# Three block products between the last layer norm's power and its use, and the third chunk's blocks fetched while the last chunk is normalised

## The chip, the cores and the metric

The kernel runs on one core of a Trainium2 chip. A core has five engines that each work through their own queue in order: TensorE (PE; its weight loads are shown as PEld), VectorE (DVE), ScalarE (ACT), GpSimd (POOL) and SyncE (SP), which issues the transfers. The metric is the device time in microseconds (us) of one execution; less is better. The kernel before took 570.78 us as the median of three runs (569.49 to 571.22).

## The reference

A transformer block on 2048 tokens of width 512, in float32: a modulated layer norm, linear attention with 32 heads, a residual, a second modulated layer norm, and a feed-forward part in which two projections to 1376 columns are multiplied and projected back.

```python
x = A_x
mod = (_silu(c) @ w_mod).reshape(c.shape[0], 6, 1, -1)
sa, ca, ga, sb, cb, gb = (mod[:, 0], mod[:, 1], mod[:, 2], mod[:, 3], mod[:, 4], mod[:, 5])
h = _layernorm(x, axis=-1) * (1 + ca) + sa
x = x + ga * _A_ref(h, A_wqkv, A_wo)
h = _layernorm(x, axis=-1) * (1 + cb) + sb
x = x + gb * _B_ref(h, B_w_gate, B_w_up, B_w_down)
...
def _B_ref(x, w_gate, w_up, w_down):
    g = jnp.einsum("bsd,df->bsf", x, w_gate)
    u = jnp.einsum("bsd,df->bsf", x, w_up)
    h = g * u
    return jnp.einsum("bsf,fd->bsd", h, w_down)
```

## The kernel before

The 2048 tokens are four chunks of 512, each of four tiles of 128 tokens. Every float32 matmul is done as three: each operand is split into a rounded high part and the low part that is left over, and the products high x high, high x low and low x high are added in PSUM. A split (L182 to L184) is a rounding copy on ScalarE and a subtraction on VectorE or GpSimd; it gives two tiles.

The attention runs first, chunk by chunk. Behind it stands the feed-forward part, in which the eleven column blocks f of 128 of the two projections are handled in two ways. The last three blocks (`lone`) are plain products for chunks 0 and 1. The first eight, and for chunks 2 and 3 all eleven, are done for two chunks at once by a scheme of Strassen's kind, in which seven products take the place of eight. `block` (L856 to L904) is one such block: it writes into four PSUM banks a, b, c, d and is a generator that stops after each product. The products stand in the order p1 (bank a), p5 (d), p6 (b), p2 (a), p7 (c), p3 (d), p4 (c); each is six matmuls of 128 x 512 at L838. Between them stand copies from bank to bank or to a tile on ScalarE (L843): a to b after p1, d to a tile after p5, b to c and b to a tile after p6; additions on VectorE: L893 after p7, L897 after p3; and two multiplications (L866), of bank a after p3 and of bank c after p4. The product of p1 of the next block goes into bank a again. The results of these multiplications are split in the next block after its p1 (`flush`), into tiles kh and kl.

The list `at` in `ffn` (L972 to L1013) hangs other work on the points: at p6 the scaling of the down weights (L985); at p7 the loads of the weights two blocks ahead, and the splits of the weights of the next block (`high` on ScalarE, L817 and L820, four operations; `lows` on GpSimd, L824, four operations); at p3 the split of the down weights; at p4 on GpSimd the sums of the weights two blocks ahead (L806, four operations). After some blocks a group of products with the down weights follows (L914 to L916), and VectorE adds its results to x (L678).

There are 19 such blocks, numbered from 0 in the order in which they run. Blocks 0 to 7 are for chunks 0 and 1, blocks 8 to 18 for chunks 2 and 3. The first two run mixed with the end of the attention and with the second layer norm of the last chunk: `fill(n)` advances the generator by n products, and the lines of the main program between the calls of `fill` set the order of everything else (L1142 to L1165). After that nothing is called by hand and the generator runs to its end (L1168 to L1170).

The layer norm of the last chunk, in its pieces: `y_b(15)` takes the last statistics; `rstd_of` adds epsilon on VectorE (L233) and raises to the power -1/2 on GpSimd (L234); `nmr_of` multiplies the mean by it on VectorE (L237); `xhat` normalises a tile on ScalarE (L243); `ln2_turn` transposes two columns of blocks on TensorE (L250), scales and shifts them on ScalarE (L262) and writes them to DRAM (`kept`, L264).

The left operands of blocks 8 to 18 come from chunks 2 and 3. `Left` (L743 to L779) loads four blocks of them from `kept` for each of two values of k: a11 and a12 of the third chunk, a21 and a22 of the fourth. `sum` makes s1 = a21 + a22, s3 = a11 - a21, s2 = s1 - a11 and s4 = a12 - s2 on VectorE (L756), `split` splits seven of them (ScalarE, then VectorE at L184), and `aside` writes both parts to DRAM (L772), from where `fetch` reads them shortly before block 8. These are 4 sums and 7 splits for each k, 22 steps in the list `trickle`; `some` takes one of them at each of the points p1, p5, p2, p3 and p4 of blocks 2 to 6, where block 2 begins with p2 (L992).

All buffers of a row of 128 x 512 come from one pool of 99, and transfers of one queue are issued by SP in order; a transfer whose buffer or source is not ready holds those behind it.

Of the kernel before, what the change touches and what calls it, by code (L numbers as in the profile page):

```python
# [22 lines left out]
def tile_adaln_block(  # L23
# [42 lines left out]
    def f32(ap):  # L66
        return ap.bitcast(F32)
# [7 lines left out]
    def B(tag, shape=(P, D), dt=F32):  # L75

        return T(tiles, tag, shape, dt)
# [30 lines left out]
    def load(src, tag):  # L108
        raw = B(tag, (P, *src.shape[1:]))[:src.shape[0]]
        nc.sync.dma_start(raw, src)  # L110
        return raw
# [70 lines left out]
    def split(src, h, l, low=None):  # L182
        nc.scalar.activation(h, src, AF.Copy)  # L183
        (low or nc.vector).tensor_tensor(l, src, f32(h), op=ALU.subtract)  # L184

    def split_raw(raw, shape=(P, D), low=None):
        h = B("w", shape, F32R)
        l = B("w", shape, F32R)
        split(raw, h[:raw.shape[0]], l[:raw.shape[0]], low)
        return h, l  # L190
# [23 lines left out]
    class Norm:  # L214
        def __init__(self, tiles):
            self.tiles = tiles
            self.mv = T(small, "mv", (P, NJ, 2))
            self.n = [None] * NJ
            self.ps = [None] * KD
            self.t = [None] * KD  # L220
# [312 lines left out]
    for k in range(KD):  # L533
        f = B("n")
# [81 lines left out]
    def y_b(i):  # L616
        ch, j = divmod(i, NJ)
        ps = yps.pop(i)
        nc.scalar.activation(xts[ch][j], ps, AF.Copy)
        norm2[ch].stats(j, of=ps)  # L620
# [106 lines left out]
    def ln2_turn(ch, *ks, cast=None):  # L727
        norm2[ch].transpose(*ks)
        norm2[ch].modulated(cb, sb, *ks, keep=kept[ch], cast=cast, parts=ch in PLAIN)
# [3 lines left out]
    kept = [[tc.dram_tile([P, D], F32, name=f"kept_{ch}_{k}") for k in range(KD)] for ch in range(NCH)]  # L733
# [6 lines left out]
    KH = KD // 2  # L740
    SIDE = ("a11", "s1", "s2", "a12", "s3", "a22", "s4")

    class Left:  # L743


        def __init__(self, cs, k):
            self.k = k
            self.f = {n: load(kept[c][kk], "f") for n, c, kk in (("a21", cs[1], k), ("a22", cs[1], KH + k),
                                                               ("a11", cs[0], k), ("a12", cs[0], KH + k))}

        def sum(self, *names):
            for n in names:
# [5 lines left out]
        def split(self, *names, low=None):  # L758
            for n in names:
                h, l = B("h", dt=F32R), B("h", dt=F32R)  # L760
                split(self.f.pop(n), h, l, low)
                self.done(n, h, l)

        def into(self, side):
# [10 lines left out]

        def steps(self):

            todo = [lambda n=n: self.sum(n) for n in ("s1", "s3", "s2", "s4")]
            return todo + [lambda n=n: self.split(n) for n in SIDE]  # L779

    def fetch(stash, side, *names):
        for n in names:
            side[n] = []
            for k in range(KH):
                side[n].append(tuple(B("h", dt=F32R) for _ in range(2)))
                for part, x in enumerate(side[n][k]):
                    nc.sync.dma_start(f32(x), stash[n, k, part])

    def plain_side(cs):
        t = [norm2[c].t for c in cs]  # L790
        return {"a11": t[0][:KH], "a12": t[0][KH:], "a22": t[1][KH:]}
# [58 lines left out]
    todo = []  # L850

    def flush():
        while todo:
            todo.pop(0)()

    def block(A, R, out, at):  # L856


        n, R = R.n, R.of
        a, b, c, d = (x[:n] for x in banks)  # L860

        def T2(tag):
            return B(tag)[:n]

        def mul(ps, x):
            nc.vector.tensor_tensor(x, ps, x, op=ALU.mult)  # L866
            todo.append(lambda: out.append(split_h(x, n)))

        def also(point):
            for do in at.get(point, ()):  # L870
                do()

        times(a, A["a11"], R["b11"], True)
        copy(b, a)
        flush()
        also("p1")
        yield
        times(d, A["s1"], R["t1"], True)
        p5 = T2("u")
        copy(p5, d)  # L880
        also("p5")
        yield
        times(b, A["s2"], R["t2"], False)
        copy(c, b)
        u2 = T2("u")
        copy(u2, b)
        also("p6")
        yield
        times(a, A["a12"], R["b21"], False)
        also("p2")  # L890
        yield
        times(c, A["s3"], R["t3"], False)
        nc.vector.tensor_tensor(p5, c, p5, op=ALU.add)  # L893
        also("p7")
        yield
        times(d, A["s4"], R["b22"], False)
        nc.vector.tensor_tensor(u2, d, u2, op=ALU.add)  # L897
        mul(a, u2)
        also("p3")
        yield  # L900
        times(c, A["a22"], R["t4"], False)
        mul(c, p5)
        also("p4")
        yield  # L904
# [36 lines left out]
    def right_load(n):  # L941
        if n < len(steps):
            rights[n] = Right(steps[n][1])

    def right_sums(n, on=None):
        if n < len(steps):
            rights[n].sums(on)

    def right_split(n, on=None):
        if n < len(steps):  # L950
            rights[n].high()
            rights[n].lows(on)
# [3 lines left out]
    def draw_load(n):  # L956
        if n < len(steps):
            f0, k = fts[steps[n][1]]
            draws[n] = load(w_down[f0:f0 + k, :], "raw")

    trickle = []

    def some(count):
        for _ in range(min(count, len(trickle))):
            trickle.pop(0)()
# [6 lines left out]
    def ffn():  # L972

        first_side, second_side = side, {}
        m = 0
        for g, (cs, fs) in enumerate(groups):
            last = g + 1 == len(groups) or groups[g + 1][0] != cs
            outs, ds = [], []
            A = first_side if cs == (0, 1) else second_side
            for f in fs:  # L980
                out = []
                draw = draws.pop(m)

                def scale(d=draw):
                    nc.vector.tensor_tensor(d, d, gb[:d.shape[0]], op=ALU.mult)  # L985

                at = {"p6": [scale],
                      "p7": [lambda: draw_load(m + 1), lambda: right_load(m + 2), lambda: right_split(m + 1)],
                      "p3": [lambda: ds.append(split_raw(draw, low=nc.gpsimd))],
                      "p4": [lambda: right_sums(m + 2)]}  # L990
                for point in ("p1", "p5", "p2", "p3", "p4")[2 if m == 2 else 0:]:
                    at.setdefault(point, []).append(lambda: some(some_at.get(m, 0)))  # L992
                if m + 1 < len(steps) and steps[m + 1][0] != cs:
                    at["p1"].append(lambda: fetch(stash, second_side, "a11", "s1"))
                    at["p7"].insert(0, lambda: fetch(stash, second_side, "s2", "a12", "s3"))
                elif m and steps[m - 1][0] != cs:
                    at["p1"].append(lambda: fetch(stash, second_side, "s4", "a22"))
                outs.append(out)
                yield from block(A, rights[m], out, at)
                m += 1  # L1000
                if free[0] and parts:
                    takes = [down_group(*p) for p in parts.pop(0)]
                    yield
                    for take in takes:
                        take()
            cut_at = {2: ([[0, 1, 2, 3], []], [[], [0, 1, 2, 3]]),
                      3: ([[0, 1, 2], []], [[3], [0, 1]], [[], [2, 3]])}[len((groups + groups[-1:])[g + 1][1])]
            parts.extend([(ch, i, js, outs, ds, last) for i, (ch, js) in enumerate(zip(cs, jss)) if js] for jss in cut_at)
        flush()
        while parts:  # L1010
            group = parts.pop(0)
            for p in group:
                down_group(*p, by_tile=not parts, end=not parts and p is group[-1])()  # L1013

    def fill(n):
        for _ in range(n):
            next(work, None)
# [70 lines left out]
    y_step(9)  # L1088
    side.update(plain_side((0, 1)))
    first = [Left((0, 1), k).into(side) for k in range(KH)]  # L1090
    right_load(0)
    right_load(1)
    g = gate_up(1, f0)
# [45 lines left out]
    draw_load(0)  # L1139
    stash, some_at = {}, {m: 1 for m in range(2, 7)}  # L1140
    work = ffn()
    y_step(14, seed=None)  # L1142
    fill(1)
# [8 lines left out]
    fill(2)  # L1152
    y_b(15)
    norm2[3].rstd_of()
    norm2[3].nmr_of()
    fill(2)
    norm2[3].xhat(0)
    fill(2)
    norm2[3].xhat(1)
    fill(1)  # L1160
# [2 lines left out]
    ln2_turn(3, 0, 1)  # L1163
    fill(1)
    ln2_turn(3, 2, 3)  # L1165
    for k in range(KH):
        trickle += Left((2, 3), k).aside(stash).steps()
    free[0] = True  # L1168
    for _ in work:
        pass  # L1170
# [27 lines left out]
```

## Time and profile before

| | |
|---|---|
| median of the runs | 570.78 us (569.49 to 571.22) |
| profiled execution | 570.02 us |
| its span, first to last instruction | 568.3 us |
| matmuls (PE) busy | 560.3 us, 99% |
| VectorE, ScalarE, GpSimd busy | 66%, 49%, 33% |
| transfers, mean | 104 GB/s |

The profile is one execution. In its timeline each row has the start and the length in us, the engine, the line of the program, the operation, output and inputs, the shapes and a count; in square brackets stands the idle time of the engine just before, with what ended it. In the chain of waits each row has start, length, engine, tile and line. SPq is SP's queue of transfers. Where a row counts several instructions, the length runs from the first start to the last end.

### The profile page before, as it was taken

The page shows a single profiled execution, that of the slowest core. Times are in us where ns is not written, and L with a number is a line of the kernel's source. Part 1 is how long each engine was busy: PE and PEld are TensorE (multiplying, and loading weights), DVE is VectorE, ACT ScalarE, POOL GpSimd, SP SyncE. Part 2 cuts the span into 40 slices and gives each one's busy share as a digit, 9 for nine tenths or more (in the row PEclk, how much of TensorE's full clock was granted, in tenths as well). Part 3 has the DMA queues.
Part 4 walks back from the last instruction along what each step waited for, and adds up shares of the span by engine and source line. Part 5 has one row for each costly group of instructions (what it writes and reads, how often), then busy time and mean ns, then how long its engine had stood idle before and what let it go on. Part 6 is the DMA issues. An engine that isn't in the chain of part 4 may idle for free.

```text
span 568.3 us, 7356 instructions
## 1 busy us (share of the span) xinstructions
PE 560.3 (99%) x2575; PEld 458.8 (81%) x2575; DVE 373.1 (66%) x614; ACT 279.8 (49%) x500; POOL 186.2 (33%) x191
## 2 busy tenths in 40 slices
PE   8999999999999999999989999999999999999997
PEld 6778888888888878878878888787888888888886
DVE  7876868868768876759767777745554434344445
ACT  3785857546456546445865545534333333334110
POOL 2000000000011300000579666665667446556200
PEclk9999999999999999999999999999999999999999
DMA  8900223302301000804208553599336012200004
GB/s 289 374 3 2 74 75 110 114 0 62 93 0 47 29 1 37 260 0 149 57 2 277 180 190 104 202 348 330 115 111 178 26 57 55 57 19 2 0 1 148
DMA packets 50309, 59.34 MB, mean 104 GB/s; under 512 B 6432, under 2 KB 27168, under 8 KB 50272
## 3 DMA queue, kind: packets, MB, share of 16 engines
q1 hardware_dynamic: 50272, 58.87, 32.1%
q8 instruction: 20, 0.33, 0.2%
q14 instruction: 17, 0.14, 0.1%
HBM read 43.12 MB, written 15.73 MB: 104 GB/s over the span
## 4 chain that ended last, share of the span: by engine, by line
PE 89%; DMA 3%; issue 2%; POOL 1%; DVE 1%; ACT 1%; SPq 1%; POOLq 0%; ACTq 0%
PE bank L838 28%; PE acc L914 6%; PE acc L915 6%; PE acc L916 6%; PE acc L614 6%; PE bank L198 5%; PE bank L196 5%; PE bank L197 5%; PE acc L329 3%; PE acc L327 3%; PE acc L328 3%; PE bank L693 2%; PE bank L691 2%; PE bank L692 2%; PE bank L250 2%
## 5 line engine op out<-in xcount | busy, mean ns | idle before, releaser
L838 PE MATMUL bank<-h,w 128*128 128x512 f32 (+1 forms) x798 | 185.5, 390 | 1.8 <-ACT bank L843 1.2
L838 PEld LDWEIGHTS bank<-h,w 128*128 128x128 f32 (+1 forms) x798 | 148.2, 186 | 35.3 <-ACT bank L843 1.7
L843 ACT ACTIVATE bank<-bank 128x512 f32<-128x512 f32 (+1 forms) x38 | 22.1, 583 | 144.8 <-PE bank L838 144.8
L678 DVE TENSOR_TENSOR x<-acc,x 128x512 f32<-128x512 f32 (+1 forms) x73 | 49.1, 684 | 49.0 <-PE acc L916 48.2
L824 POOL TENSOR_TENSOR w<-raw,w 128x256 fp32r<-128x256 f32 (+3 forms) x38 | 42.4, 1117 | 106.4 <-ACT w L817 86.4
L184 POOL TENSOR_TENSOR w<-raw,w 128x512 fp32r<-128x512 f32 (+1 forms) x25 | 34.9, 1399 | 116.0 <-DVE mv L226 87.6
L914 PE MATMUL acc<-w,kh 128*128 128x512 f32 (+2 forms) x154 | 59.6, 387 | 0.0
L915 PE MATMUL acc<-w,kh 128*128 128x512 f32 (+2 forms) x154 | 59.6, 387 | 0.0
L916 PE MATMUL acc<-w,kl 128*128 128x512 f32 (+2 forms) x154 | 59.5, 386 | 0.0
L234 POOL TENSOR_TENSOR rstd<-ve,half 128x4 f32<-128x4 f32 (+1 forms) x9 | 9.4, 1044 | 126.0 <-DVE ve L233 124.5
L184 DVE TENSOR_TENSOR kl<-u,kh 128x512 fp32r<-128x512 f32 (+1 forms) x38 | 26.8, 746 | 33.1 <-ACT kh L183 31.2
L824 POOL TENSOR_TENSOR w<-t,w 128x512 fp32r<-128x512 f32 (+1 forms) x38 | 48.4, 1293 | 0.0
L196 PE MATMUL bank<-w,h 128*128 128x512 f32 x112 | 45.0, 402 | 0.0
L198 PE MATMUL bank<-w,h 128*128 128x512 f32 x112 | 43.9, 392 | 0.0
L197 PE MATMUL bank<-w,h 128*128 128x512 f32 x112 | 43.6, 389 | 0.0
L614 PE MATMUL acc<-w,xh 128*128 128x512 f32 x120 | 38.1, 399 | 0.0
L914 PEld LDWEIGHTS acc<-w,kh 128*128 128x128 f32 (+1 forms) x154 | 28.9, 188 | 6.0
L916 PEld LDWEIGHTS acc<-w,kl 128*128 128x128 f32 (+1 forms) x154 | 28.9, 188 | 5.9
L915 PEld LDWEIGHTS acc<-w,kh 128*128 128x128 f32 (+1 forms) x154 | 28.9, 188 | 5.9
L893 DVE TENSOR_TENSOR u<-bank,u 128x512 f32<-128x512 f32 (+1 forms) x19 | 13.1, 690 | 30.0 <-PE bank L838 30.0
L243 ACT ACTIVATE n<-x,nmr,rstd 128x512 f32<-128x512 f32 x32 | 24.1, 804 | 17.2 <-DVE nmr L237 15.9
L262 ACT ACTIVATE f<-bank,col,col 128x512 f32<-128x512 f32 x28 | 20.7, 775 | 14.5 <-PE bank L250 12.4
(177 smaller groups left out, 1105.1 us busy)
## 6 DMA issues: line engine op xcount, KB each, us to landing
raw<-in_w_mod_dram SPq DMA_DIRECT2D x24, 256.0 KB, 3.7
raw<-in_B_w_down_dram SPq DMA_DIRECT2D x20, 256.0 KB, 2.9
raw<-in_B_w_gate_dram SPq DMA_DIRECT2D x36, 128.0 KB, 3.7
raw<-in_B_w_up_dram SPq DMA_DIRECT2D x36, 128.0 KB, 3.6
x<-in_A_x_dram SPq DMA_DIRECT2D x16, 256.0 KB, 5.4
kept<-f SPq DMA_DIRECT2D x16, 256.0 KB, 2.0
f<-kept SPq DMA_DIRECT2D x16, 256.0 KB, 4.8
side_s<-h SPq DMA_DIRECT2D x16, 256.0 KB, 2.6
```

Source lines behind the costliest of these rows:

```text
L184: (low or nc.vector).tensor_tensor(l, src, f32(h), op=ALU.subtract)
L196: nc.tensor.matmul(ps, ah, bh, start=i == 0, stop=False)
L197: nc.tensor.matmul(ps, ah, bl, start=False, stop=False)
L198: nc.tensor.matmul(ps, al, bh, start=False, stop=i == n - 1)
L243: nc.scalar.activation(self.n[j], self.tiles[j], AF.Identity, scale=self.rstd[:, j:j + 1], bias=self.nmr[:, j:j + 1])
L614: nc.tensor.matmul(yps[i], x, y, start=False, stop=k == KD - 1 and x is al, skip_group_check=True)
L678: nc.vector.tensor_tensor(xt[:, a:b], dn[j][:, a:b], xt[:, a:b], op=ALU.add)
L824: sub = lambda out, x, y: (on or nc.gpsimd).tensor_tensor(out, x, f32(y), op=ALU.subtract)
L838: mm = lambda x, y, **kw: nc.tensor.matmul(ps, x[:, k], y, skip_group_check=True, **kw)
L914: nc.tensor.matmul(ps, hh[:, a:b], dh[:n, c:d], start=i == 0, stop=False)
L915: nc.tensor.matmul(ps, hh[:, a:b], dl[:n, c:d], start=False, stop=False)
L916: nc.tensor.matmul(ps, hl[:, a:b], dh[:n, c:d], start=False, stop=i == len(hs) - 1)
```

## The change

Three edits. The main program calls `fill(3)` between `rstd_of` and `nmr_of` of the last norm and `fill(1)` behind `nmr_of`, where it called `fill(2)` once; so 16 products rather than 14 are called by hand before the 22 steps begin. `Left` no longer loads when it is made: `get` does, and for the third and fourth chunk a11 and a12 are fetched behind the first `xhat`, a21 and a22 at the place where all were fetched. The 22 steps are put in another order: first the four splits of a11 and a12, then for each k the sums and the other splits, and one of the five points moves from p2 to p6.

```diff
+            self.of = {"a21": (cs[1], k), "a22": (cs[1], KH + k), "a11": (cs[0], k), "a12": (cs[0], KH + k)}
+            self.f = {}
+
+        def get(self, *names):
+            for n in names:
+                c, k = self.of[n]
+                self.f[n] = load(kept[c][k], "f")
...
-                split(self.f.pop(n), h, l, low)
+                split(self.f[n], h, l, low)
...
-            todo = [lambda n=n: self.sum(n) for n in ("s1", "s3", "s2", "s4")]
-            return todo + [lambda n=n: self.split(n) for n in SIDE]
+            late = [lambda n=n: self.sum(n) for n in ("s1", "s3", "s2", "s4")]
+            late += [lambda n=n: self.split(n) for n in SIDE if n not in ("a11", "a12")]
+            return [lambda n=n: self.split(n) for n in ("a11", "a12")], late
...
-                for point in ("p1", "p5", "p2", "p3", "p4")[2 if m == 2 else 0:]:
+                for point in ("p1", "p5", "p6", "p3", "p4")[2 if m == 2 else 0:]:
...
     first = [Left((0, 1), k).into(side) for k in range(KH)]
+    for x in first:
+        x.get("a21", "a22", "a11", "a12")
...
     norm2[3].rstd_of()
+    fill(3)
     norm2[3].nmr_of()
-    fill(2)
+    fill(1)
     norm2[3].xhat(0)
+    second = [Left((2, 3), k).aside(stash) for k in range(KH)]
+    for x in second:
+        x.get("a11", "a12")
     fill(2)
     norm2[3].xhat(1)
...
     ln2_turn(3, 2, 3)
-    for k in range(KH):
-        trickle += Left((2, 3), k).aside(stash).steps()
+    for x in second:
+        x.get("a21", "a22")
+    for part in zip(*[x.steps() for x in second]):
+        for todo_k in part:
+            trickle += todo_k
     free[0] = True
```

More of the change, by code (lines that the diff above doesn't have):

```diff
@@ L747, in __init__ @@
             self.k = k
-            self.f = {n: load(kept[c][kk], "f") for n, c, kk in (("a21", cs[1], k), ("a22", cs[1], KH + k),
-                                                               ("a11", cs[0], k), ("a12", cs[0], KH + k))}
+            self.of = {"a21": (cs[1], k), "a22": (cs[1], KH + k), "a11": (cs[0], k), "a12": (cs[0], KH + k)}
[4 more added lines that the diff above has]
+                self.f[n] = load(kept[c][k], "f")
         def sum(self, *names):
```

## The prediction

> **What bounds the kernel now.** I read four views in this order: the page's busy shares, TensorE's own waits, the chain of work that ended last, and the timeline of each engine around the last layer norm.
>
> ```profile
> span 568.3 us, 7356 instructions
> ...
> PE 560.3 (99%) x2575; PEld 458.8 (81%) x2575; DVE 373.1 (66%) x614; ACT 279.8 (49%) x500; POOL 186.2 (33%) x191
> ...
> L838 PE MATMUL bank<-h,w 128*128 128x512 f32 (+1 forms) x798 | 185.5, 390 | 1.8 <-ACT bank L843 1.2 <-DVE u L866 0.3 <-DVE u L893 0.3
> ```
>
> TensorE is busy for 99% of the span, and the change leaves its 2575 matmuls as they are. A gain can only be idle time, and the third line shows that the block products (L838) idle at three places, 1.8 us in all. I look at these places next, since every edit lies there.
>
> ```profile
> 280.68 4.24 PE L838 MATMUL bank<-h,w 128*128 128x512 f32 x18
> ...
> 285.23 5.72 PE L838 MATMUL bank<-h,w 128*128 128x512 f32 x24 [0.31 <-DVE u L866]
> ...
> 292.19 3.02 PE L838 MATMUL bank<-h,w 128*128 128x512 f32 x12 [1.24 <-ACT bank L843]
> ...
> 298.09 9.83 PE L838 MATMUL bank<-h,w 128*128 128x512 f32 x42
> ...
> 313.20 9.68 PE L838 MATMUL bank<-h,w 128*128 128x512 f32 x42
> ```
>
> The last row is an undisturbed block: 42 matmuls whose last takes 0.39 us, so one starts every (9.68 - 0.39)/41 = 0.227 us. I count the loss from start to start, which also holds the slow first matmuls after a wait. After the 18 matmuls from 280.68 the next was due at 280.68 + 18 x 0.227 = 284.77 and came at 285.23: 0.46 us lost at the hand-over from block 0 to block 1. After the 24 from 285.23 it was due at 290.68 and came at 292.19: 1.51 us lost. The first edit touches this wait. The chain of waits tells where it comes from:
>
> ```profile
> 287.46 1.02 POOL rstd L234
> 288.50 0.69 DVE nmr L237
> 289.19 0.61 DVE u L866
> ...
> 290.37 0.80 ACT n L243
> 291.17 0.48 ACT u L843
> 291.64 0.50 ACT bank L843
> ...
> 292.19 3.02 PE bank L838 x12
> ```
>
> ```profile
> 283.67 0.69 DVE L897 TENSOR_TENSOR u<-bank,u 128x512 f32<-128x512 f32 x1 [0.74 <-PE bank L838]
> ...
> 284.39 0.69 DVE L866 TENSOR_TENSOR u<-bank,u 128x512 f32<-128x512 f32 x1
> ...
> 285.94 0.34 DVE L233 TENSOR_SCALAR ve<-mv 128x4 f32<-128x4 f32 x1
> ...
> 288.50 0.69 DVE L237 SCALAR_TENSOR_TENSOR nmr<-mv,rstd 128x4 f32<-128x4 f32 x1 [2.23 <-POOL rstd L234]
> ...
> 286.95 0.58 ACT L843 ACTIVATE bank<-bank 128x512 f32<-128x512 f32 x1 [3.43 <-PE bank L838]
> ...
> 289.83 0.63 ACT L183 ACTIVATE kh<-u 128x512 fp32r<-128x512 f32 x1 [1.76 <-DVE u L866]
> ...
> 291.10 1.17 POOL L806 TENSOR_TENSOR t<-raw,t 128x256 f32<-128x256 f32 x1
> ```
>
> VectorE reaches the tiny nmr operation with 2.23 us to wait, because GpSimd runs the power (L234) behind the low parts of a weight. Behind nmr stands block 0's second product on VectorE (L866), behind that the second kh on ScalarE, behind that the first normalised tile (L243) and two copies; the second copy fills the bank of block 1's p7.
>
> **The change, part by part.** *The power's three products* (p4 of block 0, p1 and p5 of block 1) now stand between L234 and nmr. On VectorE L866 follows L233 directly, at 286.3. The kh pair follows on ScalarE's 286.95 copy, at 287.4 and 288.0. The copy of p5's bank then starts at 288.5, and the copy for p7 needs only p6: its last matmul starts at 285.23 + 17 x 0.227 = 289.09, and by the 286.95 copy (p1's last matmul starts at 286.37) a copy starts 0.58 later: 289.67, done 290.25. TensorE wants it at 290.68, so the 1.51 us go, with 0.4 us to spare. nmr itself now runs behind the two kl subtractions. Even if these take the 1.97 us they take today it is issued near 290.3, and ScalarE's copies hold the first normalised tile until 290.7 anyway; so nmr costs nothing there.
>
> ```profile
> 289.72 1.97 DVE L184 TENSOR_TENSOR kl<-u,kh 128x512 fp32r<-128x512 f32 x2
> ...
> 292.54 2.21 ACT L243 ACTIVATE n<-x,nmr,rstd 128x512 f32<-128x512 f32 x3
> ...
> 294.66 0.41 ACT L817 ACTIVATE w<-raw 128x256 fp32r<-128x256 f32 x1
> ...
> 294.96 1.14 ACT L820 ACTIVATE w<-t 128x512 fp32r<-128x512 f32 x2
> ...
> 297.05 2.77 ACT L262 ACTIVATE f<-acc,col,col 128x512 f32<-128x512 f32 x4
> ```
>
> *What becomes late next: the hand-over from block 1 to block 2.* The calls that advance the products rise from 14 to 16, so p4 of block 1 and p1 of block 2 now follow each other with no transposes between, as at block 0 to 1 today. The bank of p1 is read by L866, which waits for L897, which waits for p3. Today: L897 starts 0.49 after p3's last matmul (280.68 + 11 x 0.227 = 283.18), L866 0.72 later, TensorE 0.84 after that. After the change p7 starts at 290.68, p3's last matmul at 290.68 + 11 x 0.227 = 293.18; that gives 293.67, 294.39 and 295.23, where p1 was due at 290.68 + 18 x 0.227 = 294.77. New loss: 0.46 us, and all of TensorE's queue stands behind it. Today's run from p7 to block 2 (292.19 to 298.09) held the same 18 matmuls and both groups of transposes: 5.90 - 18 x 0.227 = 1.81 us of transposes, which now come inside block 2.
>
> *ScalarE between p7 of block 1 and p7 of block 2* has the tightest cover. From 290.7 it runs one tile (0.70 each, from the 2.21 row), four high parts (0.30 from L817's start to L820's, then 3 x 0.52 from the 1.14 row, the third part not before GpSimd's L806 ends at 292.27), a tile, a weight's high part (0.52) and two tiles: done at 296.1, where the transposes start at 295.23 + 6 x 0.227 = 296.59. Then come a copy at 296.95 (0.49, from the starts in the chain), two kh (0.52 as the high parts), four L262 (0.67 each, from the 2.77 row) with a copy among them (0.49), and the copy that block 2's p7 needs: issued 301.65, done 302.23, wanted at 295.23 + 24 x 0.227 + 1.81 = 302.49. Cost 0, margin 0.26; one more ScalarE operation of 0.5 would cost 0.25.
>
> *The early fetch.* Four loads of 256 KB move ahead of block 1's weight loads on SP's queue, and four stay behind the writes of the last normalised blocks.
>
> ```profile
> 275.66 0.46 SPq L800 DMA_DIRECT2D raw<-in_B_w_up_dram  x1
> ...
> 300.26 4.20 SPq L110 DMA_DIRECT2D f<-kept  x8
> ...
> 304.80 0.77 DVE L756 TENSOR_TENSOR s<-f,f 128x512 f32<-128x512 f32 x1 [0.38 <-DMA f<-kept]
> ...
> 300.84 0.74 POOL L806 TENSOR_TENSOR t<-raw 128x256 f32<-128x256 f32 x1
> ...
> 304.56 0.38 SPq L110 DMA_DIRECT2D raw<-in_B_w_down_dram  x1
> ...
> 312.03 0.75 POOL L806 TENSOR_TENSOR t<-raw 128x256 f32<-128x256 f32 x1
> ```
>
> SP issued block 1's weights by 275.66 and GpSimd took them at 300.84; four more issues of about 0.5 us are hidden by 20 us. The 0.38 us wait of VectorE for the first sum goes, but TensorE did not wait for it: worth 0. The last L262 moves from 299.8 to 301.7, so the remaining loads end near 306 and block 2's weight loads follow them, 2 us later than 304.56. GpSimd took these at 312.03 because it was busy until then, and their high parts are due at block 3's p7, at 313.20 - 1.05 + 24 x 0.227 = 317.6. Cost 0; without that cover, up to 2 us once.
>
> *The order of the 22 steps.* As many sums and splits as before, one per point. Moving a point from p2 to p6 changes no queue, since p2 issues nothing on ScalarE or VectorE. But the order decides which blocks have splits at p1, p5 and p6 together: today (the third at p2) blocks 4 and 6, afterwards blocks 4 and 6 again, with other tiles; block 2 gets a split at p6 in place of a sum. Such a block runs a race before p4:
>
> ```profile
> 334.51 0.69 DVE L184 TENSOR_TENSOR h<-s,h 128x512 fp32r<-128x512 f32 x1 [0.22 <-ACT h L183]
> ...
> 334.79 1.01 POOL L824 TENSOR_TENSOR w<-raw,w 128x256 fp32r<-128x256 f32 x1 [5.54 <-ACT w L817]
> ...
> 364.83 0.74 POOL L824 TENSOR_TENSOR w<-raw,w 128x256 fp32r<-128x256 f32 x1 [5.52 <-ACT w L817]
> ...
> 364.90 1.22 DVE L184 TENSOR_TENSOR h<-f,h 128x512 fp32r<-128x512 f32 x1 [0.64 <-ACT w L817]
> ...
> 366.04 0.68 DVE L893 TENSOR_TENSOR u<-bank,u 128x512 f32<-128x512 f32 x1
> ...
> 358.14 8.35 PE L838 MATMUL bank<-h,w 128*128 128x512 f32 x36
> ...
> 366.77 1.65 PE L838 MATMUL bank<-h,w 128*128 128x512 f32 x6 [0.28 <-DVE u L893]
> ```
>
> In block 4 VectorE's subtraction started before GpSimd's first low part and took 0.69 us; in block 6 it started 0.07 us after it, took 1.22, and the add that p4 waits for was late: due 358.14 + 36 x 0.227 = 366.31, came 366.77, 0.46 lost. The Trainium skill (SBUF — State Buffer, "Who interferes with whom") states that a VectorE instruction with two SBUF inputs and a GpSimd instruction that reads SBUF block each other, the first to start holding the port to its end. By that rule each lost race costs most of GpSimd's 0.74 us; these rows agree, and it speaks against the new split in block 2, by 0.46 in the sum if that race were lost too. Bounds: none to five blocks lose (those with a step at p6), 0 to 2.30 us against 0.46 today. I take one, as today: 0.
>
> *Sum.* -1.51 + 0.46 = -1.05 us. The profiled execution took 570.02 us, 1.7 more than its span: 568.97. The median shown is 570.78, 0.76 above it; the same step from there gives 569.73, and I forecast 569.7, since a median will be compared.
>
> **The rivals.** *No race is lost*: a further 0.46, 569.3. Block 4 speaks for it, block 6 against it. *Two are lost, or the copy of block 2's p7 comes late by its margin and more*: 0.46 back, 570.2; the 0.26 us margin speaks for it. *Slower: GpSimd wins the race in every block with a step at p6*: blocks 2 to 6, 5 x 0.46 less today's one, 1.84 back: 570.78 - 1.05 + 1.84 = 571.6. It decides from four lost races on. Against it: in blocks 3 and 5 the step is a sum, which waits for no ScalarE result and can run before GpSimd begins. *The change does not do what it says*: nmr or a kl subtraction keeps L866 or the copies late, the 1.51 stays and the new hand-over comes on top: 571.2. Against it: L866 no longer stands behind anything that waits for GpSimd.
>
> **How the numbers follow.** Forecast 0.45, no race 0.20, two 0.15, slower 0.10, not done 0.10. Single runs lie 1.29 below to 0.44 above the shown median, so I put 1.3 below the forecast (568.4) and end at the not-done rival (571.3); the likeliest's own range is 569.1 to 570.3. What can be told from no change is about 0.3%, 1.71 us: below 569.07 or above 572.49. No case reaches either by itself; the no-race case with the spread below, and a fifth of the forecast, give 0.18 for faster. Slower needs the slower rival with the spread above, or a wait I have not seen: 0.06.
>
> **What would show it.** Right: no wait of L838 for a copy of L843 near 291; a wait of about 0.3 us for L866 near 295; nmr without an idle stretch before it; the normalised tiles about 2 us earlier at first and the last L262 about 2 us later. Wrong: a wait for L843 in block 2, waits for L893 in blocks 2, 3 or 5, transposes waiting for L243, or POOL's sums waiting for weight loads with ScalarE behind them.

## The result, and the profile after

The changed kernel takes 568.54 us as the median of seven runs (568.25 to 568.78). The kernel before, measured beside it, took 569.97 (seven runs, 569.49 to 571.22). The ratio is 0.9973, with a 95% interval of 0.9961 to 0.9984: 0.27% faster, with an interval that leaves out no change, though just inside the 0.3% that the prediction took as the least that can be told. In a later session, among 35 runs of both, it was 568.27 against 570.87, ratio 0.9963 (0.995 to 0.9975).

The code behind the diff stands six lines lower: L844 is the old L838, L849 the old L843, L872 the old L866, L899 the old L893, L903 the old L897, L826 the old L820. The page of the changed kernel shows its span, the busy shares, and the group of the block products with its idle time:

```profile
span 567.1 us, 7355 instructions
...
PE 559.5 (99%) x2575; PEld 458.2 (81%) x2575; DVE 372.2 (66%) x614; ACT 279.8 (49%) x500; POOL 186.7 (33%) x191
...
L844 PE MATMUL bank<-h,w 128*128 128x512 f32 (+1 forms) x798 | 185.1, 390 | 0.6 <-DVE u L872 0.6
```

The idle time of 1.8 us is down to 0.6, and of the three releasers one is left. TensorE's timeline shows where:

```profile
281.05 4.24 PE L844 MATMUL bank<-h,w 128*128 128x512 f32 x18
...
285.60 9.80 PE L844 MATMUL bank<-h,w 128*128 128x512 f32 x42 [0.31 <-DVE u L872]
...
295.71 1.63 PE L844 MATMUL bank<-h,w 128*128 128x512 f32 x6 [0.31 <-DVE u L872]
...
300.22 7.06 PE L844 MATMUL bank<-h,w 128*128 128x512 f32 x30
...
312.56 9.68 PE L844 MATMUL bank<-h,w 128*128 128x512 f32 x42
...
357.49 9.73 PE L844 MATMUL bank<-h,w 128*128 128x512 f32 x42
372.50 9.68 PE L844 MATMUL bank<-h,w 128*128 128x512 f32 x42
...
387.46 9.83 PE L844 MATMUL bank<-h,w 128*96 128x512 f32 x42
```

The wait for the copy at 292.19 is gone: 42 matmuls run through from 285.60. In its place stands a second wait for L872 at 295.71, and the wait in block 6 (366.77 before) is gone as well, since the row from 357.49 now holds all 42. The other engines, in rows of the same timeline:

```profile
286.54 0.68 DVE L872 TENSOR_TENSOR u<-bank,u 128x512 f32<-128x512 f32 x1
...
290.00 0.58 ACT L849 ACTIVATE bank<-bank 128x512 f32<-128x512 f32 x1 [0.56 <-PE bank L844]
...
290.23 0.70 DVE L237 SCALAR_TENSOR_TENSOR nmr<-mv,rstd 128x4 f32<-128x4 f32 x1
...
302.11 0.62 ACT L849 ACTIVATE bank<-bank 128x512 f32<-128x512 f32 x1
...
311.76 0.74 POOL L812 TENSOR_TENSOR t<-raw 128x256 f32<-128x256 f32 x1 [0.77 <-DMA raw<-in_B_w_up_dram]
...
313.98 0.74 POOL L812 TENSOR_TENSOR t<-raw,t 128x256 f32<-128x256 f32 x1
...
315.33 1.29 DVE L184 TENSOR_TENSOR kl<-u,kh 128x512 fp32r<-128x512 f32 x2 [1.88 <-ACT kh L183]
...
363.94 0.68 DVE L184 TENSOR_TENSOR h<-f,h 128x512 fp32r<-128x512 f32 x1
...
364.17 1.05 POOL L830 TENSOR_TENSOR w<-raw,w 128x256 fp32r<-128x256 f32 x1 [5.75 <-ACT w L823]
```

L872 runs at 286.54, 2.65 us ahead of the 289.19 at which the old L866 ran, nmr (L237) follows later without a wait, and the copy for p7 is done at 290.58, before TensorE needs it. The later rows are read below.

**A measure that leaves the start out.** Block 0 started at 280.68 before and at 281.05 after, though nothing ahead of it changed. The table therefore gives, for each profiled execution of this study, the start of block 0, that of block 8 (the first with 128*96 weights) and the time between, in which all edits lie. Before, blocks 7 and 8 began here:

```profile
373.72 9.68 PE L838 MATMUL bank<-h,w 128*128 128x512 f32 x42
...
388.68 9.83 PE L838 MATMUL bank<-h,w 128*96 128x512 f32 x42
```

| kernel | median (range) | ratio to before | profiled | block 0 | block 8 | between |
|---|---|---|---|---|---|---|
| before | 569.97 to 570.90 in five sessions | | 570.02 | 280.68 | 388.68 | 108.00 |
| changed | 568.54 (568.25-568.78) | 0.9973 | 568.78 | 281.05 | 387.46 | 106.41 |
| changed, again (e0) | 568.27 (568.06-569.28) | 0.9963 | 568.22 | 280.54 | 386.92 | 106.38 |
| e1 first edit alone | 573.48 (572.55-575.11) | 1.0051 | 572.55 | 281.23 | 391.22 | 109.99 |
| e2 fetch and order alone | 569.89 (569.30-570.18) | 0.9980 | 569.91 | 281.16 | 388.58 | 107.42 |
| e3 nmr at its old place | 569.72 (569.06-570.48) | 0.9981 | 570.11 | 281.60 | 388.81 | 107.21 |
| e4 one product ahead of nmr | 568.65 (568.29-570.32) | 0.9967 | 568.49 | 280.78 | 387.17 | 106.39 |
| e5 a11, a12 fetched late | 570.82 (569.96-573.32) | 1.0003 | 570.73 | 281.10 | 389.34 | 108.24 |
| e6 block 6 without p2 | 571.11 (570.06-572.23) | 1.0008 | 570.08 | 280.81 | 388.76 | 107.95 |
| e7 block 2 begins with p5 | 569.35 (567.76-570.29) | 0.9972 | 568.31 | 280.84 | 386.65 | 105.81 |
| e10 the same kernel as e7 | one run | | 569.39 | 281.53 | 387.52 | 105.99 |
| e8 sums behind p4 | 569.78 (569.04-570.56) | 0.9980 | 570.21 | 281.50 | 388.90 | 107.40 |
| e9 first edit, sums behind p4 | 570.93 (569.14-571.65) | 0.9997 | 570.25 | 281.63 | 388.90 | 107.27 |
| e12 e9 with the early fetch | 568.99 (568.11-569.30) | 0.9962 | 568.99 | 281.27 | 387.67 | 106.40 |

Between the two blocks the changed kernel is 1.59 us shorter in its profiled execution. Of these, 1.01 lie ahead of block 3 (it starts 32.52 us after block 0 before, 31.51 after), where the prediction had 1.51 less 0.46, so 1.05. The other 0.57 lie in block 6 (from its start to that of block 7 15.58 us before, 15.01 after), where the prediction had 0.

### The profile page after: what moved, and what is told of

The parts are those of the page before. It is cut to its first block, busy times and chain, and to the rows that moved or that the text cites. A ratio compares the mean times of both kernels' runs of the same rounds, so it can differ in the third digit from the quotient of the medians.

```text
span 567.1 us, 7355 instructions
## 1 busy us (share of the span) xinstructions
PE 559.5 (99%) x2575; PEld 458.2 (81%) x2575; DVE 372.2 (66%) x614; ACT 279.8 (49%) x500; POOL 186.7 (33%) x191
## 4 chain that ended last, share of the span: by engine, by line
PE 95%; DMA 3%; DVE 1%; SPq 1%; issue 0%; DVEq 0%
PE bank L844 32%; PE acc L614 7%; PE acc L920 6%; PE acc L921 6%; PE acc L922 6%; PE bank L198 5%; PE bank L196 5%; PE bank L197 5%; PE acc L329 3%; PE acc L328 3%; PE acc L327 3%; PE bank L693 2%; PE bank L691 2%; PE bank L692 2%; PE bank L250 2%; DMA raw<-in_A_wqkv_dram 2%
## 5 line engine op out<-in xcount | busy, mean ns | idle before, releaser
L844 PE MATMUL bank<-h,w 128*128 128x512 f32 (+1 forms) x798 | 185.1, 390 | 0.6 <-DVE u L872 0.6
L844 PEld LDWEIGHTS bank<-h,w 128*128 128x128 f32 (+1 forms) x798 | 148.3, 186 | 33.7 <-issue 0.7
L849 ACT ACTIVATE bank<-bank 128x512 f32<-128x512 f32 (+1 forms) x38 | 22.2, 583 | 145.7 <-PE bank L844 145.7
L899 DVE TENSOR_TENSOR u<-bank,u 128x512 f32<-128x512 f32 (+1 forms) x19 | 13.1, 691 | 30.1 <-PE bank L844 27.0
L243 ACT ACTIVATE n<-x,nmr,rstd 128x512 f32<-128x512 f32 x32 | 24.2, 804 | 17.2 <-DVE nmr L237 17.2
L183 ACT ACTIVATE w<-raw 128x512 fp32r<-128x512 f32 (+2 forms) x44 | 26.4, 618 | 2.8 <-DMA raw<-in_A_wqkv_dram 1.8
```

Of the source, the lines that this page charges most:

```text
L844: mm = lambda x, y, **kw: nc.tensor.matmul(ps, x[:, k], y, skip_group_check=True, **kw)
```

## The experiments

**The parts of the change, one at a time.** First the calls of `fill` alone (e1):

```diff
     norm2[3].rstd_of()
+    fill(3)
     norm2[3].nmr_of()
-    fill(2)
+    fill(1)
```

> The first edit alone: three products between power and nmr, one behind it; the fetch and the order of the 22 steps as before. My theory: the 1.51 us wait for the copy into p7's bank goes and the hand-over to block 2 costs 0.46, but block 2 now comes before its blocks from DRAM: the first sum at p2 still needs a21 and a22, whose loads stand behind the last writes. In the changed kernel these loads were issued from 302.76 us; landing some 3 us later puts the sum near 306 to 307.6, L893 behind it, and p4 of block 2, due at 305.7, near 308 to 309: a new wait of 2.5 to 3.5 us for L893. Total 571.5 to 572.5, slower than before. Rival: the edits are independent and the loads are hidden anyway: 569.97 - 1.51 + 0.46 = 568.9.

It took 573.48 us, ratio 1.0051 (1.0036 to 1.0067): half of the change, and slower than before. Its timeline in block 2, VectorE and TensorE:

```profile
307.17 1.64 DVE L756 TENSOR_TENSOR s<-f,f 128x512 f32<-128x512 f32 x1 [4.91 <-DMA f<-kept]
308.73 0.68 DVE L893 TENSOR_TENSOR u<-bank,u 128x512 f32<-128x512 f32 x1
...
309.46 1.66 PE L838 MATMUL bank<-h,w 128*128 128x512 f32 x6 [3.32 <-DVE u L893]
```

The first sum (L756) waits 4.91 us for the blocks written and read back some 2 us later than before; L893, which p4 needs, stands behind it on VectorE, and TensorE waits 3.32. The rival, that the first edit does its work alone, falls. The profiled execution (572.55) is what was expected; the median is 0.93 above it. The five other executions were granted a clock of 0.994 to 0.997, the profiled one 1.0; why is open. The other two edits without the first (e2):

```diff
     norm2[3].rstd_of()
-    fill(3)
     norm2[3].nmr_of()
-    fill(1)
+    fill(2)
```

> The other two edits alone: early fetch and new order of the steps, the calls of fill as before. My theory: they move TensorE by nothing but the race of block 6. The 1.51 us wait for the copy near 291 stays, the hand-over to block 2 stays covered by transposes, and the 0.46 us wait for L893 in block 6 stays or goes: 569.5 to 570.0. Rival (the new order is what brings the gain): below 569.0, with no wait for the copy.

569.89 us, ratio 0.998 (0.9972 to 0.9989), as expected. The old wait is all there, and in block 6 there is none:

```profile
292.67 3.02 PE L844 MATMUL bank<-h,w 128*128 128x512 f32 x12 [1.24 <-ACT bank L849]
```

**What must stand ahead of nmr.** Two kernels move nmr against the products: right behind the power with all four products after it (e3), and with one product ahead (e4).

```diff
e3:
     norm2[3].rstd_of()
-    fill(3)
     norm2[3].nmr_of()
-    fill(1)
+    fill(4)
...
e4:
     norm2[3].rstd_of()
-    fill(3)
+    fill(1)
     norm2[3].nmr_of()
-    fill(1)
+    fill(3)
```

> The changed kernel with nmr directly behind the power, where it was, and all four products ahead of the first normalised tile. My theory: half of the 1.51 us came from nmr ahead of L866 and half from the first normalised tile ahead of the copies on ScalarE. With the tile moved, the copy for p7 ends near 291.4 where 290.68 is due: a wait of 0.7 to 0.9 us comes back, total about 569.4. Rival A (only the place of the tile counts): as the changed kernel, 568.5. Rival B (only nmr counts): the whole 1.5 us back, 570.1.

> The changed kernel with one product between power and nmr and three behind it. My theory: what has to stand ahead of nmr on VectorE is only L866, the multiplication of bank c behind p4; nmr may then wait for GpSimd with nothing urgent behind it but the kl subtractions. As the changed kernel: 568.5, no wait for the copy. Rival (all three products are needed to outlast the power): a wait for L849 of 0.3 to 0.8 us near 291, 568.9 to 569.3.

With nmr at its old place L872 stands behind it again, and a part of the wait is back:

```profile
292.39 4.37 PE L844 MATMUL bank<-h,w 128*128 128x512 f32 x18 [0.52 <-ACT bank L849]
```

It is 0.52 and not 1.24, since here the copies do not stand behind a normalised tile. So the 1.51 us had two causes, nmr ahead of L866 on VectorE and the first tile (L243) ahead of the copies on ScalarE; e3 takes away the second alone. With one product ahead of nmr nothing waits (568.65, and 106.39 us between the blocks, as the changed kernel): that one product issues L872, and the two others need not stand there.

**The early fetch.** In e5 a11 and a12 are fetched where a21 and a22 are; fills and order are those of the changed kernel.

```diff
     second = [Left((2, 3), k).aside(stash) for k in range(KH)]
-    for x in second:
-        x.get("a11", "a12")
     fill(2)
...
     for x in second:
         x.get("a21", "a22")
+    for x in second:
+        x.get("a11", "a12")
```

> The changed kernel with its order of steps, but a11 and a12 loaded where all were loaded before, ahead of a21 and a22. My theory: the split of a11 in block 2 waits for a load that SP issues only behind the last writes, from about 302.8 us, and that lands near 305.5; its subtraction stands ahead of L893 on VectorE, so p4 of block 2 comes near 307.7 where 305.7 is due: 2.0 us lost, total about 570.5. Rival (the early fetch is not needed): 568.5, no wait for L893 in block 2.

570.82 us, ratio 1.0003 (0.9992 to 1.0014): the gain is gone. The first split in block 2 is late, as the first sum was in e1:

```profile
306.19 0.69 DVE L184 TENSOR_TENSOR h<-f,h 128x512 fp32r<-128x512 f32 x1 [4.08 <-ACT h L183]
306.80 0.68 DVE L899 TENSOR_TENSOR u<-bank,u 128x512 f32<-128x512 f32 x1
...
307.54 1.65 PE L844 MATMUL bank<-h,w 128*128 128x512 f32 x6 [1.55 <-DVE u L899]
```

**Block 6, and a miss that led further.** The kernel before, with the step at p2 of block 6 left to the next point (e6), to see what the race there is worth:

```diff
-                for point in ("p1", "p5", "p2", "p3", "p4")[2 if m == 2 else 0:]:
+                for point in ("p1", "p5", "p3", "p4") if m == 6 else ("p1", "p5", "p2", "p3", "p4")[2 if m == 2 else 0:]:
```

> The kernel before with no step at p2 in block 6; its four steps stand at p1, p5, p3 and p4. My theory: the 0.46 us that block 6 lost came from the subtraction at p2 that VectorE ran against GpSimd's first low part. Without it L893 runs at its earliest place, the wait for L893 near 366 goes and the rest stays: 569.5. Rival (the splits at p1 and p5 make the copies on ScalarE late, and these stay): the wait for L893 stays, 570.0.

The wait in block 6 went (14.99 us from its start to that of block 7, 15.58 before), and yet the median was 571.11, ratio 1.0008 (0.9999 to 1.0018). What its profile shows in block 2 is nothing that this edit touches; up to block 6 it is the kernel before:

```profile
305.23 1.06 DVE L756 TENSOR_TENSOR s<-f,f 128x512 f32<-128x512 f32 x1 [0.79 <-DMA f<-kept]
306.21 0.68 DVE L893 TENSOR_TENSOR u<-bank,u 128x512 f32<-128x512 f32 x1
...
304.99 0.74 POOL L824 TENSOR_TENSOR w<-raw,w 128x256 fp32r<-128x256 f32 x1
...
306.94 1.65 PE L838 MATMUL bank<-h,w 128*128 128x512 f32 x6 [0.37 <-DVE u L893]
```

VectorE waited 0.41 us longer for the blocks than in the profile of before (0.79 against 0.38). By then GpSimd's first low part had begun, 0.24 us ahead of the sum, which took 1.06 us where it took 0.77 before. So L893 began 0.72 us later, and p4 of block 2 waited. In the profile of before the sum began at 304.80, ahead of GpSimd, and the rows had just met:

```profile
305.49 0.68 DVE L893 TENSOR_TENSOR u<-bank,u 128x512 f32<-128x512 f32 x1
...
304.98 1.19 POOL L824 TENSOR_TENSOR w<-raw,w 128x256 fp32r<-128x256 f32 x1
```

L893 ended there at 306.17, and p4 was due at 298.09 + 36 x 0.227 = 306.26: 0.09 us of margin behind a transfer and a race. The miss itself is not explained by this alone: the kernel before has the same steps in block 2, so by block 6 e6 should still be the shorter of the two. Either most executions of before do not lose block 6, or e6 loses elsewhere; that stays open. The next run (e8) tests whether most executions of before lose that margin: the kernel before, with the steps of block 2 at p3, p4 and p4, so that the first sum stands behind L893.

```diff
-                for point in ("p1", "p5", "p2", "p3", "p4")[2 if m == 2 else 0:]:
+                for point in ("p3", "p4", "p4") if m == 2 else ("p1", "p5", "p2", "p3", "p4"):
```

> The kernel before, with one thing changed: in block 2 the three steps are taken at p3, p4 and p4 where they were taken at p2, p3 and p4, so that the first sum (L756) stands behind the add that p4 waits for (L893). Theory: in most executions of the kernel before the first sum waits for its blocks a little longer than in the profiled one (0.38 us there, 0.79 us in the run whose block 6 had no step at p2) and makes p4 of block 2 late by 0.5 to 1 us; without it the median falls to 569.8 to 570.3 and the wait of L838 for L893 in block 2 is gone, those for L843 (1.2) and L866 (0.3) stay. Rival: the spread of the kernel before comes from elsewhere (the start), and the median stays within 0.3 of the kernel before, near 570.8.

569.78 us against 570.74, ratio 0.998 (0.9972 to 0.9989): 0.96 us less. Between the blocks its profile is 0.60 shorter, of which 0.58 is block 6 (15.00 us against 15.58), where VectorE's split now came first:

```profile
306.10 0.69 DVE L893 TENSOR_TENSOR u<-bank,u 128x512 f32<-128x512 f32 x1 [0.88 <-PE bank L838]
...
365.33 0.69 DVE L184 TENSOR_TENSOR h<-f,h 128x512 fp32r<-128x512 f32 x1 [0.29 <-ACT h L183]
...
365.61 1.02 POOL L824 TENSOR_TENSOR w<-raw,w 128x256 fp32r<-128x256 f32 x1 [5.51 <-ACT w L817]
```

L893 now waits for TensorE, not for a transfer. The other 0.36 us of the median is what the profile of before did not show. That it is block 2's wait is not shown, since block 6 went with it, and e6 leaves open how often before loses each.

**Is the early fetch needed once the sum stands elsewhere?** e9 is e8 with the `fill` calls of e1; e12 is e9 with the early fetch of a11 and a12 added, all steps still in the old order.

```diff
e12 against e9:
+    second = [Left((2, 3), k).aside(stash) for k in range(KH)]
+    for x in second:
+        x.get("a11", "a12")
     fill(2)
     norm2[3].xhat(1)
...
-    for k in range(KH):
-        trickle += Left((2, 3), k).aside(stash).steps()
+    for x in second:
+        x.get("a21", "a22")
+    for x in second:
+        trickle += x.steps()
```

> The kernel before with the first edit (three products between the power and nmr) and the three steps of block 2 at p3, p4 and p4; blocks are fetched late and in the old order. Theory: the first edit alone was slower only because the first sum, late by 3.3 us, stood ahead of the add that p4 waits for; with the sum behind it the first edit gives what it gives in the changed kernel, two waits of 0.3 us for L866 and none for L843, and the time is 568.3 to 569.1 (the wait of block 6 may come back, 0.46 us). Rival: the early fetch is worth something of its own (the late loads hold other work too), and the time is 569.5 or more with a wait behind a load in blocks 2 or 3.

> The changed kernel with its fills and its early fetch of a11 and a12, but with the steps in the old order and at the old points, and those of block 2 at p3, p4 and p4; it is the run with the first edit and the sums behind p4 (570.93, its profiled execution 570.25), with the early fetch alone added. Theory A: what that run lost against the changed kernel came from its eight late loads, behind which the weights arrive late (GpSimd's first sum of block 2 waited 3.3 us for them, against 0.77 in the changed kernel); with four of them early that wait is near 1 us and the time 568.3 to 569.1. Theory B: it came from the old order of the steps, which loses the races of VectorE and GpSimd in blocks 3 and 6 (0.29 and 0.46 us in its profiled execution); then it stays at 570 to 571, with waits for L899 in blocks 3 and 6.

e9 took 570.93 us, no faster than before (ratio 0.9997, 0.9987 to 1.0007), though the two waits of the first edit are as in the changed kernel: my theory failed and its rival held. e12 took 568.99 (0.9962, 0.9949 to 0.9976), with 106.40 us between the blocks, the changed kernel's 106.41: theory A held, and the old order of the steps lost no race in its profile. The profiles show what the late loads hold. GpSimd, VectorE and TensorE of e9 in block 3, and at the end its race in block 6:

```profile
313.14 9.97 PE L838 MATMUL bank<-h,w 128*128 128x512 f32 x42
...
313.73 0.74 POOL L806 TENSOR_TENSOR t<-raw 128x256 f32<-128x256 f32 x1 [3.31 <-DMA raw<-in_B_w_up_dram]
...
315.95 0.74 POOL L806 TENSOR_TENSOR t<-raw,t 128x256 f32<-128x256 f32 x1
...
315.98 1.86 DVE L184 TENSOR_TENSOR kl<-u,kh 128x512 fp32r<-128x512 f32 x2 [1.95 <-POOL t L806]
...
319.41 0.84 POOL L824 TENSOR_TENSOR w<-raw,w 128x256 fp32r<-128x256 f32 x1 [2.72 <-ACT w L817]
...
319.57 1.23 DVE L184 TENSOR_TENSOR h<-s,h 128x512 fp32r<-128x512 f32 x1
320.72 0.68 DVE L893 TENSOR_TENSOR u<-bank,u 128x512 f32<-128x512 f32 x1
...
365.06 0.74 POOL L824 TENSOR_TENSOR w<-raw,w 128x256 fp32r<-128x256 f32 x1 [5.62 <-ACT w L817]
...
365.14 1.20 DVE L184 TENSOR_TENSOR h<-f,h 128x512 fp32r<-128x512 f32 x1 [0.66 <-ACT w L817]
```

and of e12 (L811 is L806 of before, L829 is L824, L843 is L838):

```profile
310.86 0.96 POOL L811 TENSOR_TENSOR t<-raw 128x256 f32<-128x256 f32 x1 [0.80 <-DMA raw<-in_B_w_up_dram]
...
312.82 9.68 PE L843 MATMUL bank<-h,w 128*128 128x512 f32 x42
...
315.66 1.29 DVE L184 TENSOR_TENSOR kl<-u,kh 128x512 fp32r<-128x512 f32 x2 [1.95 <-ACT kh L183]
...
318.73 0.69 DVE L184 TENSOR_TENSOR h<-s,h 128x512 fp32r<-128x512 f32 x1
...
319.08 0.94 POOL L829 TENSOR_TENSOR w<-raw,w 128x256 fp32r<-128x256 f32 x1 [5.05 <-ACT w L822]
```

With eight late loads ahead of them on SP's queue, GpSimd waits 3.31 us for the weights of block 4. Its last sum then begins 0.03 us ahead of VectorE's two kl subtractions, which take 1.86 us where they take 1.29 with GpSimd idle. VectorE comes late to its split, GpSimd's low part has begun 0.16 us before it, and the split takes 1.23 instead of 0.69. L893 is late by that, and block 3 takes 9.97 instead of 9.68. Of the 0.87 us between e9 and e12, 0.29 is this and 0.56 is block 6 (15.56 us against 15.00), whose race e9 loses as the kernel before does; that the late loads decide that race too is not shown. By the medians, which are from two sessions, the early fetch alone is worth 1.94 us; the rest of it lies in executions that were not profiled, and stays open.

**A version without the new wait.** In e7 the hand-over of block 2 gets cover: block 2 begins with p5 in bank d, and both transpose groups stand behind p1.

```diff
-    def block(A, R, out, at):
+    def block(A, R, out, at, d_first=False):
...
+        if d_first:
+            p5 = p_5()
+            yield
...
-    fill(2)
+    fill(3)
...
+    norm2[3].transpose(2, 3)
...
-    ln2_turn(3, 2, 3)
+    norm2[3].modulated(cb, sb, 2, 3, keep=kept[3], parts=False)
```

> The changed kernel with block 2 begun by p5 instead of p1, both groups of transposes behind p1, and the scaling of the second group (two L262) behind p6's copies. My theory: bank d is read for the last time by L903, a step ahead of L872, so p5 covers the wait at the hand-over from block 1 to block 2; the transposes cover the copy of bank a. 0.46 us go, 568.1 us, with one wait of L844 for L872 left, that near 285. Rival (the hand-over is only moved: p6 waits for the copy of bank a, or the copy for p7 comes late behind L262): 568.5 or more, with a wait for L849 between 296 and 303.

The changed kernel ran once more beside it (e0):

> The changed kernel once more, beside the others: 568.5 us; two waits of L844 for L872 of 0.3 us each, no wait for L899 in blocks 4 and 6 if the race is decided the same way in every execution, one of 0.3 us if it falls differently.

It took 568.27 us, with its two waits for L872 and no others. In e7 the second of them went, and between the blocks it is the shortest of all (105.81):

```profile
285.39 12.53 PE L844 MATMUL bank<-h,w 128*128 128x512 f32 x54 [0.31 <-DVE u L872]
```

But its median is 569.35, 1.08 above the changed kernel in the same session (568.27), with runs from 567.76 to 570.29. One more execution of the same kernel (e10) was to tell why:

> A second look at the kernel whose block 2 starts with p5, of which most executions took 569 to 570 us and the profiled one 568.3. Theory: the last blocks fetched for block 8 arrive at a fixed time, since the transfers run without a gap before it, so that a kernel that is earlier there only waits: in the first look the weight load of TensorE waited 0.5 us for h from side_a at 396.1; in an execution of 569 us or more that wait is 1 to 2 us. Rival: the loss is in the races of VectorE and GpSimd in blocks 2 to 6, shown as waits of L844 for L907 of 0.3 us each; or in the start, shown as a longer wait for the first normalised tile (0.5 us in the first look).

It took 569.39 us. TensorE's timeline in block 8:

```profile
387.52 9.37 PE L844 MATMUL bank<-h,w 128*96 128x512 f32 x40
397.21 0.71 PE L844 MATMUL bank<-h,w 128*96 128x512 f32 x2 [0.32 <-DMA h<-side_a]
```

and the row of its busy times by stage (busy us and count for PE, PEld, DVE, ACT and POOL; the last three are the clock, the share of the transfer engines' time and GB/s):

```profile
375.00:396.00 21.00, 21.00 (x93) 16.28 (x93) 10.97 (x15) 9.75 (x21) 9.94 (x11) 1.00 1.05 355
```

The transfer engines are busy throughout these 21 us, and the loads of a22, the last block fetched for block 8, do not come sooner when TensorE is early: e7 starts block 8 0.81 us ahead of the changed kernel (386.65 against 387.46) and issues these loads 0.50 us behind it (389.45 against 388.95). What delays them is open; in e7 nothing was transferred from 355 to 360 us, where the changed kernel moved 52 GB/s. Of the 0.60 us gained by block 8 only 0.27 is left when block 9 begins in e7 (119.92 us after block 0, 120.19 in the changed kernel), and nothing in e10 (120.32). The wait of the weight load was expected at 1 to 2 us; in e10 it is 0.73, of which 0.32 show as a wait of the matmuls. The 1.08 us by which e10 is slower than e7 are the start of block 0 (0.69), block 8 (0.22) and block 3 (0.19, its weights waited for 1.77 us and the kl pair at 1.86 us, as in e9). So each of the three explanations has a part, and the median of e7 is not explained by one of them. No version of this study beats the changed kernel.

## Why the prediction was right, and where it was wrong

*The power's three products* (-1.51): right. L872, the kh pair, the copies and nmr came in the order worked out, within about 0.4 us of the times, and block 0 itself was 0.37 later. e3 adds that nmr was one of two causes, e4 that one product would do.

*The hand-over from block 1 to block 2* (+0.46): right. The last of the 42 matmuls from 285.60 started at 285.60 + 9.80 - 0.39 = 295.01, so the next was due at 295.24 and came at 295.71: 0.47 us. With the first step that is 1.05 forecast and 1.01 measured up to block 3.

*ScalarE's margin* of 0.26: right. The copy ran from 302.11 to 302.73, and p7 was due 12 matmuls into the row from 300.22, at 302.94: 0.21 to spare.

*The early fetch* (0): wrong, and it is the step that failed. It was priced at nothing because "TensorE did not wait for it". That was true of one execution with 0.09 us of margin; in e6 the same wait stopped TensorE. And the step was priced by itself. With the first edit the writes come 2 us later, and then the first sum without the early fetch costs 3.32 (e1), or, with the sum out of the way, e9 costs 0.87 by the profiles and 1.94 by the medians against e12, of which 0.29 is traced to the late loads. The cost that the prediction bounded there, "up to 2 us once" for late weight loads, is what the early fetch keeps away: in the changed kernel GpSimd's first sum waits 0.77 us and the fourth ends at 314.72, ahead of the kl pair at 315.33.

*The races* (0, one lost as today): the rule held, the count did not. None was lost ahead of p4 in blocks 2 to 6, which was the rival with 0.20. That gives 0.57 more, not 0.46: the price ended at p4's first matmul, and after the wait p4's six matmuls take 1.65 us, where 5 x 0.227 + 0.39 = 1.53 is the undisturbed time. The rows of before held a hint: its split waited for L817, the copy that releases GpSimd too, so that the two began together; where it waited for its own high part (L183), as in e8, it was 0.28 ahead. Why it waited for L817 is not settled.

The Trainium skill's rule (SBUF — State Buffer, "Who interferes with whom") agrees with all of these rows: the split takes 0.68 to 0.69 us when it begins first and 1.20 to 1.23 when GpSimd's low part is ahead of it.

*The sum.* -1.59 by profile instead of -1.05, taken from 570.78 as before, gives 569.2. The measured median lies another 0.65 lower, below the likeliest case's own range (569.1 to 570.3) and only 0.14 above the lower end of the whole range. That it is inside is in part luck: the lower end was there for the spread of single runs, and no step accounted for so low a median. What the rest is stays open. The kernel before was itself measured between 569.97 and 570.90 by session, and its median may hold a loss in block 2 that its profiled execution did not have and that the change takes away too. e8 speaks for it, with 0.36 us beyond its profile's gain; e6, which was not faster, leaves it open.

## What to carry to other kernels

A wait that just does not happen in the one profiled execution is not free of cost: compare the end of the late instruction with the time at which the bottleneck needs it, and where the margin is a tenth of a us behind a transfer, price it from both sides: the transfer was waited for 0.4 us longer in the one profiled execution of e6, the same program up to there. Price the edits of a change together, since one that costs nothing alone can be what another needs. And compare profiled executions between two points that enclose the edit; here the start alone differed by 1.1 us.

## What the runs showed of the hardware

The same program up to block 0 reached it between 280.54 and 281.63 us in fourteen profiled executions, a spread of 1.09 us, where the change is worth 1.59 between blocks 0 and 8.

From 375 to 396 us the transfers ran at 353 to 357 GB/s on average with all their engines busy in before, changed, e7 and e10 alike, wherever TensorE stood. The Trainium skill (DMA: Bandwidth & Descriptors, "Specifications") puts the limit of the memory for one core at about 358 GB/s; the averages lie near it, but it is no ceiling here: in the 9 us from 375 to 384 the rates were 380 GB/s before, 388 in the changed kernel, 352 in e7 and 369 in e10.
